# Linear attention and a leaky-ReLU FFN on one core: the four transposed tiles of one batch dealt out over two PSUM banks

## The chip, the cores and the metric

The kernel runs on one core of a Trainium2 chip. A time is the device time of one execution in microseconds (us), and the time of a kernel is the median of several executions. Beside these times there is one profiled execution, whose trace says for each instruction when it began, how long it took and what released it. All positions such as "73.66" are microseconds from the start of the span of that execution.

## The reference, cut to what matters

Eight batches of eight heads go through a linear attention (576 tokens, 64 features per head); the result, 4608 rows of 512 numbers, goes through two matrix products with a leaky ReLU between them.

```python
def phi(x, c, s):
    r = np.maximum(x, 0.0)
    return np.concatenate([r * c, r * s], axis=-1)
q_p, k_p = phi(q, cos_w, sin_w), phi(k, cos_w, sin_w)
kv = np.einsum('bhsf,bhsd->bhfd', k_p, v)
z = np.sum(k_p, axis=2)
num = np.einsum('bhsf,bhfd->bhsd', q_p, kv)
den = np.einsum('bhsf,bhf->bhs', q_p, z)[..., None] + 1e-06
x = (num / den).transpose(0, 2, 1, 3).reshape(B * S, H * D)
h = x @ w_in
out = np.maximum(0.01 * h, h) @ w_out
```

## The kernel before, in words

The rows are worked on in nine groups. Groups 0 to 7 are the first 512 tokens of the batches 0 to 7, as four tiles of 128 rows (`J = 4`); group 8 gathers the last 64 tokens of all batches. Group g = 2, the third batch, is the one that the change touches. For each group:

- the k and v of the batch are scaled (`k_token`, L253 on VectorE and GpSimd and L251 on ScalarE) and cast (`v_pairs`, L259 on ScalarE and L261 on the others), and `kv_sum` (L326) sums them into the 128x66 matrix of each head with 72 matmuls;
- `q_prep` scales q, a DMA transpose (L363) turns it;
- `num` (L412) multiplies tile j of q by these matrices into the PSUM tile `ps_num`, and `divide` (L423, L427, L428 on VectorE) divides and writes tile j of `xs`;
- `xs` is turned into `xT`, because the next product contracts over features. For groups 3 to 8 a DMA does it (L377). For group 2 TensorE does it, in `x_transpose(g, j, eng)`, tile by tile: four transposes of 128x128 (L389) write tile j of the PSUM tile `ps_x`, and a copy (L259, here always on ScalarE, since the entry `'xe'` of batch 2 is `'AAAA'`) brings it to `xT`;
- the first FFN product (L486 up to group 1; from group 2 on Strassen-like in seven products per unit, `ffn1s`, L638, whose sums of operands are made by `x_sum` and whose results are finished in `ffn1e`) and the second (`ffn2s`, L755, also in seven products, with sums of `g` made by `g_sum` on VectorE; all these sums have the line of the helper `tt_op`, L538).

The order of the work is written out by hand. `TUNE["O"]` is a string of units of matmuls per group, and every other step has a position on the same axis; `weave` issues a step as soon as its position is reached. What is issued after what on one engine is therefore fixed; the waits between engines are not in the code, they are derived from which instruction touches which tile. For group 2, `num` stands at positions 16.40, 17.14, 17.61 and 18.20 and `x_transpose` at 17.31, 17.68, 18.89 and 18.94. On TensorE the transposes of tile 0 to 3 (called X0 to X3 below, and their copies C0 to C3) therefore stand among the units of L755 of group 1 in this order: num 1, 4 matmuls, X0, 8 matmuls, num 2, X1, 12 matmuls, num 3, 12 matmuls, 4 matmuls, X2, X3, 12 matmuls, 4 matmuls, then the first unit of L638 of group 2.

Group 1's second FFN product runs its seven products in the order 1, 2, 6, 5, 7, 4, 3. After product 6 VectorE writes `t2` (L776), after product 7 `t3` (L778), both as a sum of a PSUM tile and `t1`; in the trace both are "ext<-ps,ext" of L538. Product 7 also needs `g_sum` number 3 ("g<-g" at 76.69), whose last part VectorE makes in this stage.

PSUM: the pool `ps_h` has two slots of two banks (a bank holds 2048 bytes per partition) for the tiles with the tag "h". `ps_x` is one of them, the chain of products 6 and 7 of group 1 another; after group 2's `x_transpose` the pool is closed, and its banks become the four tiles `ps_f0` to `ps_f3` of L638. A tile j of `ps_x` has 4 x 128 numbers of two bytes, 1024 bytes per partition, so `ps_x` fills two banks.

Of the kernel before, what the change touches and what calls it, by code (L numbers as in the profile page):

```python
# [9 lines left out]
dt = mybir.dt  # L10
# [3 lines left out]
P = 128  # L14
J = 4
# [5 lines left out]
def kernel(  # L21
# [26 lines left out]
    NKC = DM // P  # L48
# [29 lines left out]
    def psum(where, shape, dtype, name):  # L78
        p = {"h": ps_h, "o": ps_o, "n": ps_n}[where]
        return p.tile(shape, dtype, name=name, tag="ps_" + where)  # L80

    st = {}
# [5 lines left out]
    def need(*keys):  # L88
        for key in keys:
            assert key in done, key  # L90
# [166 lines left out]
    def copy(eng, o, i):  # L257
        if eng is ACT:
            nc.scalar.copy(o, i)  # L259
        else:  # L260
            eng.tensor_copy(o, i)  # L261
# [106 lines left out]
    def xT_tile(g):  # L368
        if ("xT", g) not in st:
            st["xT", g] = xtpool.tile([P, J, NKC, P], dt.float16, name="xT")  # L370
        return st["xT", g]
# [10 lines left out]
    def x_transpose(g, j, eng):  # L382

        need(("num", g, j))
        if j == 0:
            st["ps_x", g] = psum("h", [P, J, NKC, P], dt.float16, "ps_x")
        ps = st["ps_x", g][:, j]
        for c in range(NKC):
            nc.tensor.transpose(ps[:, c], st["xs", g][:, j, 2 * c : 2 * c + 2, :], ident)  # L389
        copy(eng, xT_tile(g)[:, j], ps)  # L390
        if j == J - 1:
            done.add(("xT", g))
# [488 lines left out]
    ps = psum("h", [P, 2, 512], dt.float32, "ps_numh")  # L881
# [81 lines left out]
    ps = psum("n", [P, 2, DM], dt.float32, "ps_o")  # L963
# [26 lines left out]
    ps = psum("h", [P, 2, MAIN], dt.float16, "ps_x")  # L990
# [177 lines left out]
    for b, t in TUNE["B"].items():  # L1168
# [17 lines left out]
        if isinstance(t["x"], list):  # L1186
            for j in range(J):
                at(t["x"][j], x_transpose, b, j, engines[t["xe"][j]])
        else:
            at(t["x"], x_transpose_dma, b)  # L1190
# [40 lines left out]
```

## Time and profile before

| | |
|---|---|
| median of 3 runs (lowest to highest) | 274.75 us (274.72 to 275.25) |
| the profiled execution, its own time | 275.64 us |
| its span, first instruction to last | 273.9 us |
| TensorE busy in the span | 264.3 us |
| VectorE busy | 209.3 us |
| ScalarE busy | 189.5 us |
| GpSimd busy | 114.1 us |
| granted TensorE clock, mean | 0.998 |

A row of the timeline reads: start in us, duration in us, engine, line, operation, output <- input, shape, number of instructions merged, and in brackets how long the engine sat idle before it and what ended that. PE is TensorE's matmuls, PEld its weight loads, DVE is VectorE, ACT is ScalarE, POOL is GpSimd, SPq the queue that issues most DMAs. Merged rows of matmuls carry the modelled end of the last one, which lies 0.1 to 0.2 us behind the start of the next row.

### The profile page before, as it was taken

What the parts mean: (1) busy time and instruction counts of PE and PEld (TensorE: products, weight loads), DVE (VectorE), ACT (ScalarE), POOL (GpSimd) and SP (SyncE); (2) the same over time, 40 slices, a digit from 0 to 9 for tenths busy, and PEclk for the clock granted to TensorE, in tenths of its full rate; (3) what the DMA queues carried; (4) which work ended last, traced back from release to release, by engine and by line L of the source; (5) the groups of instructions that cost most, each with busy time, mean ns of one, the idle gap of its engine ahead of it and who ended that gap; (6) DMA issues with size and microseconds to landing.
All of it is one profiled execution on the core that took longest, in us unless ns stands there. A gap on an engine that the chain in (4) does not pass through costs nothing.

```text
span 273.9 us, 7194 instructions
## 1 busy us (share of the span) xinstructions
PE 264.3 (97%) x2925; PEld 223.2 (81%) x2925; DVE 209.3 (76%) x430; ACT 189.5 (69%) x344; POOL 114.1 (42%) x93
## 2 busy tenths in 40 slices
PE   8799999999889999999999999999999999999994
PEld 3576555556779999999999999989999899999983
DVE  4760595698887899889797979886987778867652
ACT  7766537589968998988797878967857365645500
POOL 2496006992738818996693477330003001000000
PEclk9999999999999999999999999999999999999999
DMA  6999999989999499879979975847199051200314
GB/s 228 369 392 410 383 398 373 357 203 254 300 217 364 117 207 272 237 248 191 253 255 213 306 226 174 181 118 149 45 123 224 2 115 42 77 14 29 112 43 115
DMA packets 75040, 57.08 MB, mean 208 GB/s; under 512 B 47232, under 2 KB 63616, under 8 KB 74624
## 3 DMA queue, kind: packets, MB, share of 16 engines
q1 hardware_dynamic: 74400, 56.11, 73.8%
q10 hardware_dynamic: 608, 0.52, 0.6%
q8 instruction: 23, 0.38, 0.6%
q14 instruction: 9, 0.07, 0.1%
HBM read 36.70 MB, written 9.44 MB: 168 GB/s over the span
## 4 chain that ended last, share of the span: by engine, by line
PE 88%; DMA 3%; ACT 3%; DVE 1%; POOL 1%; SPq 1%; issue 1%; ACTq 0%
PE ps L755 32%; PE ps_f L638 31%; PE ps_h L486 10%; PE ps_o L512 5%; PE ps_kv L326 4%; DMA kst<-in_k_dram 3%; PE ps_num L412 3%; ACT qp L251 1%; PE ps_f L755 1%; POOL kp L253 1%; PE ps_qt L398 1%; ACT xT L259 1%; PE ps_xth L464 1%; PE ps_x L389 0%; SPq L135 0%
## 5 line engine op out<-in xcount | busy, mean ns | idle before, releaser
L755 PEld LDWEIGHTS <-g 128*128 128x128 f16 x640 | 61.5, 98 | 7.0 <-ACT g L665 0.2
L755 PE MATMUL ps<-w,g 128*128 128x256 f16 x496 | 65.4, 273 | 0.0
L665 ACT ACTIVATE g<-ps_f 128x512 f16<-128x512 f32 x84 | 48.3, 596 | 17.4 <-DVE ps_f L538 10.7
L638 PEld LDWEIGHTS <-w 128*128 128x128 f16 x448 | 48.7, 114 | 1.8 <-DVE ext L538 0.6
L638 PE MATMUL ps_f<-xT,w 128*128 128x256 f16 x336 | 48.7, 273 | 0.5 <-DVE ext L538 0.3
L638 PEld LDWEIGHTS <-wext 128*128 128x128 f16 x336 | 36.3, 114 | 0.7
L755 PE MATMUL ps<-T,ext 128*128 128x256 f16 x240 | 31.9, 273 | 0.0
L486 PE MATMUL ps_h<-xT,w 128*128 128x512 f16 (+1 forms) x144 | 28.9, 355 | 0.1
L253 POOL TENSOR_SCALAR kp<-kst,cos_t 128x256 f16<-128x256 f32 (+1 forms) x20 | 26.8, 1346 | 4.9 <-DMA kst<-in_k_dram 3.6
L755 PEld LDWEIGHTS <-ext 128*128 128x128 f16 x256 | 24.6, 98 | 2.6
L638 PE MATMUL ps_f<-X,wext 128*128 128x256 f16 x176 | 26.5, 273 | 0.0
L253 POOL TENSOR_SCALAR kp<-kst,sin_t 128x256 f16<-128x256 f32 x16 | 21.4, 1346 | 11.7 <-ACT ext L774 6.4
L486 PEld LDWEIGHTS <-w 128*128 128x128 f16 x144 | 16.0, 114 | 10.8
L538 DVE TENSOR_TENSOR ps_f<-ps_f,u 128x512 f32<-128x512 f32 x28 | 19.4, 694 | 6.4 <-ACT u L259 4.2
L538 DVE TENSOR_TENSOR y<-ps_f,s 128x512 f32<-128x512 f32 x28 | 19.2, 686 | 4.6 <-PE ps_f L638 3.4
L538 DVE TENSOR_TENSOR osb<-ps,ext 128x512 f32<-128x512 f32 x23 | 15.8, 687 | 7.2 <-PE ps L755 7.1
L259 ACT COPY u<-ps_f 128x512 f32<-128x512 f32 x25 | 14.7, 587 | 8.9 <-PE ps_f L638 8.6
L428 DVE TENSOR_TENSOR xs<-ps_num,rden 128x512 f16<-128x512 f32 x28 | 19.4, 691 | 1.0
L496 ACT ACTIVATE g<-ps_h 128x1024 f16<-128x1024 f32 x16 | 15.8, 1023 | 6.1 <-PE ps_h L486 6.1
L665 ACT ACTIVATE g<-y 128x512 f16<-128x512 f32 x28 | 17.7, 632 | 3.1 <-DVE y L538 3.1
L755 PE MATMUL ps<-ext,g 128*128 128x256 f16 x128 | 18.1, 273 | 0.0
L259 ACT COPY ps_f<-ps_f 128x512 f32<-128x512 f32 x24 | 13.7, 573 | 5.2 <-PE ps_f L638 4.5
(117 smaller groups left out, 464.4 us busy)
## 6 DMA issues: line engine op xcount, KB each, us to landing
out_dram<-osb SPq DMA_DIRECT2D x32, 256.0 KB, 2.8
qst<-in_q_dram SPq DMA_DIRECT2D x7, 1024.0 KB, 9.4
kst<-in_k_dram SPq DMA_DIRECT2D x6, 1152.0 KB, 9.5
vst<-in_v_dram SPq DMA_DIRECT2D x5, 1152.0 KB, 7.5
w2st<-in_moe_w_out_dram SPq DMA_DIRECT2D x3, 1024.0 KB, 11.9
vst<-in_v_dram SPq DMA_DIRECT2D x4, 576.0 KB, 8.0
ext<-in_moe_w_in_dram SPq DMA_DIRECT2D x4, 512.0 KB, 9.6
kst<-in_k_dram SPq DMA_DIRECT2D x2, 576.0 KB, 8.5
```

Of the source, the lines that this page charges most:

```text
L253: eng.tensor_scalar(out=o, in0=i, scalar1=0.0, scalar2=col, op0=ALU.max, op1=ALU.mult)
L259: nc.scalar.copy(o, i)
L326: nc.tensor.matmul(ps[:, o, (c - lo) * NE : (c - lo + 1) * NE], lhsT=st["kp", b][sl, c, j, :], rhs=vm[sl, c, j, :], start=(j == 0), stop=( ...
L412: nc.tensor.matmul(ps[lo:hi, h // 4, (h % 4) * NE : (h % 4 + 1) * NE], lhsT=qpT[:, h, lo:hi], rhs=kv[b][:, h, :],)
L428: nc.vector.tensor_tensor(out=xs, in0=ps[:, :, 0 : 4 * NE].rearrange("p a (b e) -> p a b e", e=NE)[:, :, :, 0:D], in1=rden.rearrange("p (a ...
L486: nc.tensor.matmul(ps[:, m % 2, lo:hi], lhsT=w1[m // 4, c][0][:, w1[m // 4, c][1], m % 4 : 512 : 4], rhs=xT[:, lo // P : hi // P, c, :], s ...
L496: nc.scalar.activation(st["g", g][:, m - 1 : m + 1, :], ps, AF.Lrelu)
L512: nc.tensor.matmul(st["ps_o", g, tt], lhsT=st["g", g][:, m, tt * P : (tt + 1) * P], rhs=w2[:, m, :], start=(m == 0), stop=(m == NFT - 1),)
L538: eng.tensor_tensor(out=o, in0=a, in1=b, op=op)
L638: nc.tensor.matmul(ps[:, mi * HT : (mi + 1) * HT], lhsT=a[:, c, 2 * r0 + mi : 512 : 4], rhs=b[:, c], start=(n in (1, 5) and mi == 0 and c ...
L665: nc.scalar.activation(st["g", g][:, m : m + 2, r * HT : (r + 1) * HT], {"a": A, "c": y22, "e": E, "d": B_}[e].rearrange("p (m t) -> p m t ...
L755: nc.tensor.matmul(ps[:, tt], lhsT=a[:, i, tt * P : (tt + 1) * P], rhs=b[:, i], start=(first and i == 0), stop=(i == NPR - 1 and (apart or ...
```

## The change

Two lines of `x_transpose` change. Tile j of `ps_x` was at offset j x 1024 bytes, so that tiles 0 and 1 lay in the first bank of its slot and tiles 2 and 3 in the second. It is now at bank j % 2, half j // 2: tiles 0 and 2 lie in the first bank, tiles 1 and 3 in the second. Size of the tile, instructions, their order and their engines stay as they were.

```diff
         if j == 0:
-            st["ps_x", g] = psum("h", [P, J, NKC, P], dt.float16, "ps_x")
-        ps = st["ps_x", g][:, j]
+            st["ps_x", g] = psum("h", [P, 2, J // 2, NKC, P], dt.float16, "ps_x")
+        ps = st["ps_x", g][:, j % 2, j // 2]
         for c in range(NKC):
             nc.tensor.transpose(ps[:, c], st["xs", g][:, j, 2 * c : 2 * c + 2, :], ident)
         copy(eng, xT_tile(g)[:, j], ps)
```

## The prediction

> **What bounds the kernel now.** I read the page first: the span, and the chain that ended last.
>
> ```profile
> span 273.9 us, 7194 instructions
> PE ps L755 32%; PE ps_f L638 31%; PE ps_h L486 10%; PE ps_o L512 5%; PE ps_kv L326 4%; DMA kst<-in_k_dram 3%; PE ps_num L412 3%; ACT qp L251 1%; PE ps_f L755 1%; POOL kp L253 1%; PE ps_qt L398 1%; ACT xT L259 1%; PE ps_xth L464 1%; PE ps_x L389 0%; SPq L135 0%
> ```
>
> The chain is TensorE nearly throughout; "ACT xT L259" with 1% is the copy out of `ps_x`, so the stage of the change lies on it. Next I took the timeline of TensorE there, and one row of its weight loads.
>
> ```profile
> 72.01 0.42 PE L412 MATMUL ps_num<-kv,qpT 128*128 128x66 f16 x8
> 73.66 0.38 PE L389 MATMUL ps_x<-ident,xs 128*128 128x128 f16 x4 [1.24 <-ACT xT L259]
> 73.88 1.47 PE L755 MATMUL ps<-T,ext 128*128 128x256 f16 x12
> 75.19 0.42 PE L412 MATMUL ps_num<-kv,qpT 128*128 128x66 f16 x8
> 75.45 1.47 PE L755 MATMUL ps<-T,ext 128*128 128x256 f16 x12
> 76.76 0.60 PE L755 MATMUL ps<-w,g 128*128 128x256 f16 x4
> 77.19 0.39 PE L389 MATMUL ps_x<-ident,xs 128*128 128x128 f16 x4
> 78.25 0.38 PE L389 MATMUL ps_x<-ident,xs 128*128 128x128 f16 x4 [0.67 <-ACT xT L259]
> ...
> 80.73 0.63 PE L638 MATMUL ps_f<-xT,w 128*128 128x256 f16 x4 [0.35 <-DVE ext L538]
> ...
> 82.16 1.32 PE L326 MATMUL ps_kv<-vm,kp 64*128 64x66 f16 x72
> ```
> ```profile
> 72.23 0.10 PEld L389 LDWEIGHTS <-xs 128*128 128x128 f16 x1
> ```
>
> Three gaps stand here. X1 (73.66) and X3 (78.25) wait for a copy on ScalarE, and the first unit of group 2 (80.73) waits for VectorE. The weights of X1 were loaded at 72.23, so its `xs` was ready 1.4 us before it ran: it waited for C0 alone, although C0 reads bytes that X1 doesn't write. X2 (77.19), the first tile of the other bank, didn't wait. That fits a wait per bank, though it doesn't prove one (rival B).
>
> ScalarE's rows say why the copies are late.
>
> ```profile
> 73.05 0.56 ACT L259 COPY xT<-ps_x 128x512 f16<-128x512 f16 x1
> ...
> 74.72 0.56 ACT L259 COPY xT<-ps_x 128x512 f16<-128x512 f16 x1
> ...
> 77.61 0.58 ACT L259 COPY xT<-ps_x 128x512 f16<-128x512 f16 x1 [1.52 <-PE ps_x L389]
> 78.67 0.58 ACT L259 COPY xT<-ps_x 128x512 f16<-128x512 f16 x1 [0.47 <-PE ps_x L389]
> ...
> 79.96 1.14 ACT L259 CAST vm<-vst 128x1152 f16<-128x1152 f32 x1
> ```
>
> C0 (73.05) and C1 (74.72) have no idle time ahead of them: they stand behind other work of ScalarE, which the change leaves where it is. C2 and C3 do wait, for X2 and X3. So the second half is a ping-pong: X2, C2, X3, C3, each after the other. VectorE's rows show what runs beside it.
>
> ```profile
> 73.51 0.58 DVE L253 TENSOR_SCALAR kp<-kst,sin_t 128x256 f16<-128x256 f32 x1
> 74.95 0.69 DVE L538 TENSOR_TENSOR ext<-ps,ext 128x512 f32<-128x512 f32 x1 [0.86 <-PE ps L755]
> ...
> 76.08 0.69 DVE L428 TENSOR_TENSOR xs<-ps_num,rden 128x512 f16<-128x512 f32 x1
> 76.69 0.41 DVE L538 TENSOR_TENSOR g<-g 128x512 f16<-128x512 f16 x1
> 77.03 1.22 DVE L538 TENSOR_TENSOR g<-g,ext 128x2048 f16<-128x2048 f16 x1
> 78.16 0.35 DVE L253 TENSOR_SCALAR kp<-kst,cos_t 128x256 f16<-128x256 f32 x1
> 79.29 0.42 DVE L538 TENSOR_TENSOR X<-xT 128x512 f16<-128x512 f16 x1 [0.78 <-ACT xT L259]
> 79.63 0.35 DVE L253 TENSOR_SCALAR kp<-kst,sin_t 128x256 f16<-128x256 f32 x1
> 79.98 0.69 DVE L538 TENSOR_TENSOR ext<-ps,ext 128x512 f32<-128x512 f32 x1
> ```
>
> VectorE is idle twice between 73.51 and 79.98: 0.86 us before `t2` (74.95), for the matmuls held up behind X1, and 0.78 us before the sum X (79.29), for C3. Then it makes `t3` (79.98), which frees the PSUM bank that the unit at 80.73 takes. The end of this stage is thus set by VectorE, and that is where the gain must be read, not at TensorE's gaps.
>
> **The change part by part.** Nothing is added or taken out, and no step is moved in any queue; only waits change. Removed: X1 after C0, X3 after C2. New: X2 after C0, X3 after C1.
>
> First gap. X1 follows num 2 at the pitch of num 3 and its successor (75.19 to 75.45, 0.26): 72.27 instead of 73.66, 1.39 earlier. The 12 matmuls behind it go to 72.49. `t2` began 1.07 behind their first (73.88 to 74.95), which would be 73.56, but VectorE is free only at 74.95 - 0.86 = 74.09. So `t2` moves by 0.86, not by 1.39. Behind it VectorE had no gap: xs 3 ends at 76.77 - 0.86 = 75.91, the sum of g (76.69) at 77.10 - 0.86 = 76.24.
>
> Second gap. TensorE's row: num 3 at 73.80, the 4 matmuls of product 7 (76.76) at 75.37, after `t2`'s end at 74.78. X2 follows at 77.19 - 1.39 = 75.80; its new wait, C0, ended at 73.61. X3 follows 0.22 later (73.66 to 73.88 is the pitch of four transposes) at 76.02: xs 3 is there at 75.91, and its new wait, C1, ended at 75.28, 0.74 earlier. Behind X3 stand 12 matmuls of product 7, at 76.24, then 4 more; their sum of g is there at 76.24. So the new waits cost nothing here, with 0.7 us to spare, and X3 comes 2.23 us earlier.
>
> What is late next. C2 starts 0.42 after X2 (77.19 to 77.61), at 76.22; ScalarE is free at 77.61 - 1.52 = 76.09. C3 starts at C2's end at the latest, 76.80, and ends at 77.38, before VectorE is through with the row at 78.16, which it left at 79.29 - 0.78 = 78.51 and would now leave at 77.65. The sum X then starts at 77.65 instead of 79.29: both idle times are gone, 0.86 + 0.78 = **1.64 us**. `t3` starts at 79.98 - 1.64 = 78.34; product 7's 12 matmuls end at 76.24 + 1.47 = 77.71, in time. The unit at 80.73 goes to 79.09. TensorE itself could have been 2.23 earlier; 0.59 of that becomes a longer wait for `t3`.
>
> Behind it. `kv_sum` (82.16) would go to 80.52. It needs the cast of v (79.96), which follows C3 by 1.29: 78.09 to 79.23. This half of v comes from a load that stands ahead of the change in SP's queue and doesn't move; the row behind it in that queue are q's transposes, and the last row is from the view of the DMA issues for this stretch (count, KB, us from issue to landing):
>
> ```profile
> 72.86 0.46 SPq L135 DMA_DIRECT2D vst<-in_v_dram  x1
> 73.49 5.77 SPq L363 DMA_TRANSPOSE qpT<-qp  x2
> ```
> ```profile
> vst<-in_v_dram SPq DMA_DIRECT2D x1, 576.0 KB, 4.5
> ```
>
> It lands at 72.86 + 4.5 = 77.36, 0.73 before the cast. From 82 on TensorE is full, and this row of the view by windows (its last three numbers are the granted clock, the DMA engines' busy share and GB/s) has the DMA engines 60% busy, so a backlog of loads that could not move up with the rest is worked off there:
>
> ```profile
> 86.00:92.00 6.00, 6.00 (x73) 5.48 (x71) 5.76 (x16) 5.64 (x12) 6.00 (x4) 1.00 0.60 230
> ```
>
> So the 1.64 us reach the end, bar what follows.
>
> The unknown cost is overlap with GpSimd. VectorE's sums move up into its last scaling of k:
>
> ```profile
> 75.70 1.13 POOL L253 TENSOR_SCALAR kp<-kst,sin_t 128x256 f16<-128x256 f32 x1
> ```
> ```profile
> 58.23 2.60 POOL L253 TENSOR_SCALAR kp<-kst,sin_t 128x256 f16<-128x256 f32 x1
> ```
> ```profile
> 58.45 1.21 DVE L538 TENSOR_TENSOR ext<-w,T 128x2048 f16<-128x2048 f16 x1
> ```
>
> At 58.45 VectorE took 1.21 for such a sum inside an operation of GpSimd, and 1.22 at 77.03 outside one; GpSimd's took 2.60 instead of 1.13. So GpSimd pays, and 75.70 + 2.60 = 78.30 is well before `kv_sum` at 80.52. But VectorE's scaling took 0.58 at 73.51 beside GpSimd and 0.35 at 78.16 alone, and the latter would now start at 77.30, possibly still beside it. Bounds: 0 (no overlap left) to 0.23 for that row, or 1.00 for the sum of g if it is held until GpSimd ends (75.70 + 1.13 = 76.83, instead of 76.69 - 0.86 = 75.83). A gain is excluded, since no operation of VectorE here gets less of GpSimd beside it than before. I take 0.10 in all, nearer to the pair at 58 us than to the upper ends.
>
> The Trainium skill speaks against this move: "SBUF — State Buffer", section "Who interferes with whom", says that a VectorE instruction with two SBUF inputs contends with a GpSimd one that reads SBUF, and that whichever issues second is blocked until the first is done. By it the sum of g would be the one held, and the gain would be that of rival A; the rows at 58 us show the opposite side paying.
>
> Writing one bank of `ps_x` while ScalarE reads the other is new as well, and no row shows it for this tile. If it cost nothing, the times above hold; if it cost everything, X1 would be held until C0's end and X3 until C2's, which is rival B's time. I take nothing: the two groups of 12 matmuls (73.88 and 75.45) both took 1.47, the first while C1 read another bank.
>
> Sum: 1.64 - 0.10 = **1.54 us**. The profiled execution, 275.64 with a span of 273.9, would become 274.1 with 272.4. It lies 0.89 above the median of the timed runs, and what lies around the span is not touched, so I take the difference over: 274.75 - 1.54 = **273.2 us**.
>
> **The rivals.**
>
> A, GpSimd's share. The sum of g is held by the scaling that began at 75.70, for 1.00. VectorE has no gap left to hide it, so the gain is 1.64 - 1.00 = 0.64, **274.1 us** (the 0.23 alone would leave 1.41, within the forecast). For it: the 0.58 at 73.51. Against it: the pair at 58 us, where the same kinds of operation met and VectorE lost nothing.
>
> B, the change doesn't do what it says. The waits are derived, and the trace before would look the same if they were per tile of PSUM: C1 ended at 75.28, so that X2 at 77.19 would have shown no wait for it either. Then X1 still waits for C0 and X3 for C2, and the time stays at **274.75 us**. For it: X1's wait is certainly coarser than the bytes. Against it: the bank is the next unit above the bytes, and every idle time of the stage is told by it.
>
> The Trainium skill's "PSUM — Partial Sum Buffer", section "PSUM bank collisions raise a hardware error", asks that PSUM be guarded by bank and quadrant and found two engines on different banks clean, so that a guard by whole tiles would be wider than needed; nothing in the trace tells which one was built here.
>
> C, slower: the half of v comes too late. The transposes of q stand right behind its load in SP's queue, and TensorE's own progress frees the buffer that the second one fills (`num` of group 2 reads it), so it may start up to 1.39 earlier and share the DMA engines with the load. A landing past 78.09 delays the cast; past 80.52 - 1.14 = 79.38 it delays `kv_sum` beyond its new time; the point from which the kernel is slower than before is a landing past 82.16 - 1.14 = 81.02, 8.2 us after its issue. Price, an estimate: shared half and half for its whole length the load takes 2 x 4.5 = 9.0, lands at 81.86, and `kv_sum` starts at 83.00, 0.84 late: **275.6 us**. For it: the two do overlap from 73.49 on. Against it: only 1.39 of the 4.5 can be newly shared, which ends at 78.75, not at 81.02.
>
> **How the numbers follow.** Forecast (a gain of 1.1 to 2.2): 0.68. A (0.55 to 1.1): 0.12. B: 0.10. C: 0.08. The remaining 0.02 is a gain above TensorE's own 2.23. The forecast's own range is 272.5 to 273.65, its ends being TensorE's 2.23 in place of VectorE's 1.64 and half of the 1.00 lost. For 8 in 10 A must be in: 272.4 to 274.2, with 0.1 below for the spread of a median. It leaves out B and C, 0.18. A measurement of this kernel can tell about 0.2%, 0.55 us, from no change. Faster by more than that: 0.68 + 0.12 + 0.02 = 0.82; within: B, 0.10; slower: C, 0.08.
>
> **What would show it.** Right: X1 and X3 with no idle time for "ACT xT" ahead of them, X1 about 0.26 behind num 2, C2 and C3 back to back, no longer each behind its transposes, VectorE without its 0.86 and 0.78, the wait for `t3` at the first L638 grown to about 0.9, that unit near 79.1 and `kv_sum` near 80.5. Wrong: waits at X1 or X3 as before (B); "g<-g" or the scalings of VectorE longer by tenths (A); an idle time of ScalarE for the DMA of v ahead of its cast (C). It would also be wrong if the gain stood at 80 us but was gone at the end: then a later stage, not this one, waits for something that didn't move up.

## The result: no measurable difference, and the same waits as before

| | before | changed |
|---|---|---|
| median (lowest to highest), 13 runs each | 275.15 us (274.72 to 275.94) | 274.99 us (274.67 to 275.64) |
| the profiled execution | 275.64 us | 274.91 us |
| its span | 273.9 us | 273.1 us |

The ratio is 0.9999, with a 95% interval of 0.9989 to 1.0008: the change is worth between 0.3 us faster and 0.2 us slower. The forecast of 273.2 us, with a range of 272.4 to 274.2, was wrong. The time is that of rival B. (B's own figure, 274.75, was the median of three runs; over 13 runs the kernel before came to 275.15.)

The timeline of the changed kernel shows it without any arithmetic. TensorE first, from X0 (70.20) to the first unit of group 2:

```profile
70.20 0.39 PE L389 MATMUL ps_x<-ident,xs 128*128 128x128 f16 x4
70.43 1.04 PE L755 MATMUL ps<-T,ext 128*128 128x256 f16 x8
71.30 0.42 PE L412 MATMUL ps_num<-kv,qpT 128*128 128x66 f16 x8
72.89 0.38 PE L389 MATMUL ps_x<-ident,xs 128*128 128x128 f16 x4 [1.17 <-ACT xT L259]
...
76.42 0.39 PE L389 MATMUL ps_x<-ident,xs 128*128 128x128 f16 x4
77.48 0.38 PE L389 MATMUL ps_x<-ident,xs 128*128 128x128 f16 x4 [0.67 <-ACT xT L259]
...
79.95 0.63 PE L638 MATMUL ps_f<-xT,w 128*128 128x256 f16 x4 [0.35 <-DVE ext L538]
```

X1 still sits idle for 1.17 us and X3 for 0.67, both released by "ACT xT", the copies. ScalarE's copies C0 and C3 of the same execution:

```profile
72.27 0.56 ACT L259 COPY xT<-ps_x 128x512 f16<-128x512 f16 x1
...
77.90 0.58 ACT L259 COPY xT<-ps_x 128x512 f16<-128x512 f16 x1 [0.47 <-PE ps_x L389]
```

C0 ends at 72.27 + 0.56 = 72.83 and X1 starts at 72.89, though X1 now writes the second bank and C0 reads the first. TensorE's 1.17 us of idle time began at 71.72, so that 0.55 us of it were over before C0 had begun (72.27). No conflict in PSUM can account for that part; a fixed order, X1 after C0, does. VectorE's two idle times, the terms of the forecast's sum, are there as before:

```profile
74.18 0.69 DVE L538 TENSOR_TENSOR ext<-ps,ext 128x512 f32<-128x512 f32 x1 [0.91 <-PE ps L755]
...
78.51 0.42 DVE L538 TENSOR_TENSOR X<-xT 128x512 f16<-128x512 f16 x1 [0.78 <-ACT xT L259]
```

From X0 to the first unit of L638 the stage takes 79.95 - 70.20 = 9.75 us. Before, X0 stood at

```profile
70.91 0.39 PE L389 MATMUL ps_x<-ident,xs 128*128 128x128 f16 x4
```

and the stage took 80.73 - 70.91 = 9.82. This length is used below for all kernels, since it is free of what happens ahead of X0 and behind the stage.

### The profile page after: what moved, and what is told of

Same layout as the page of the kernel before. It is cut to its first block, busy times and chain, and to the rows that moved or that the text cites. A ratio compares the mean times of both kernels' runs of the same rounds, so it can differ in the third digit from the quotient of the medians.

```text
span 273.1 us, 7194 instructions
## 1 busy us (share of the span) xinstructions
PE 263.2 (96%) x2925; PEld 222.9 (82%) x2925; DVE 209.2 (77%) x430; ACT 189.5 (69%) x344; POOL 114.8 (42%) x93
## 4 chain that ended last, share of the span: by engine, by line
PE 89%; DMA 3%; ACT 3%; DVE 1%; POOL 1%; SPq 1%; issue 1%; ACTq 0%
PE ps L755 33%; PE ps_f L638 32%; PE ps_h L486 10%; PE ps_o L512 5%; PE ps_kv L326 4%; DMA kst<-in_k_dram 3%; PE ps_num L412 3%; ACT qp L251 1%; PE ps_f L755 1%; POOL kp L253 1%; PE ps_qt L398 1%; ACT xT L259 1%; PE ps_xth L464 1%; PE ps_x L389 0%; SPq L135 0%
## 5 line engine op out<-in xcount | busy, mean ns | idle before, releaser
L755 PEld LDWEIGHTS <-g 128*128 128x128 f16 x640 | 61.5, 98 | 6.9 <-ACT g L665 0.2
L755 PE MATMUL ps<-w,g 128*128 128x256 f16 x496 | 65.4, 273 | 0.0
L638 PEld LDWEIGHTS <-w 128*128 128x128 f16 x448 | 48.7, 114 | 1.9 <-DVE ext L538 0.6
L638 PE MATMUL ps_f<-xT,w 128*128 128x256 f16 x336 | 48.8, 273 | 0.5 <-DVE ext L538 0.3
L638 PEld LDWEIGHTS <-wext 128*128 128x128 f16 x336 | 36.3, 114 | 0.7
L755 PE MATMUL ps<-T,ext 128*128 128x256 f16 x240 | 31.9, 273 | 0.0
L253 POOL TENSOR_SCALAR kp<-kst,cos_t 128x256 f16<-128x256 f32 (+1 forms) x20 | 25.9, 1303 | 4.1 <-DMA kst<-in_k_dram 2.8
L253 POOL TENSOR_SCALAR kp<-kst,sin_t 128x256 f16<-128x256 f32 x16 | 22.8, 1432 | 10.6 <-PE ps_kv L326 5.3
L755 PEld LDWEIGHTS <-ext 128*128 128x128 f16 x256 | 24.6, 98 | 2.5
L638 PE MATMUL ps_f<-X,wext 128*128 128x256 f16 x176 | 26.5, 273 | 0.0
L538 DVE TENSOR_TENSOR ps_f<-ps_f,u 128x512 f32<-128x512 f32 x28 | 19.4, 694 | 6.5 <-ACT u L259 4.3
L538 DVE TENSOR_TENSOR y<-ps_f,s 128x512 f32<-128x512 f32 x28 | 19.2, 687 | 4.8 <-PE ps_f L638 3.6
L538 DVE TENSOR_TENSOR osb<-ps,ext 128x512 f32<-128x512 f32 x23 | 15.8, 688 | 7.2 <-PE ps L755 7.1
L428 DVE TENSOR_TENSOR xs<-ps_num,rden 128x512 f16<-128x512 f32 x28 | 19.4, 692 | 1.0
L755 PE MATMUL ps<-ext,g 128*128 128x256 f16 x128 | 18.1, 273 | 0.0
```

Of the source, the lines that this page charges most:

```text
L253: eng.tensor_scalar(out=o, in0=i, scalar1=0.0, scalar2=col, op0=ALU.max, op1=ALU.mult)
L428: nc.vector.tensor_tensor(out=xs, in0=ps[:, :, 0 : 4 * NE].rearrange("p a (b e) -> p a b e", e=NE)[:, :, :, 0:D], in1=rden.rearrange("p (a ...
L538: eng.tensor_tensor(out=o, in0=a, in1=b, op=op)
L638: nc.tensor.matmul(ps[:, mi * HT : (mi + 1) * HT], lhsT=a[:, c, 2 * r0 + mi : 512 : 4], rhs=b[:, c], start=(n in (1, 5) and mi == 0 and c ...
L755: nc.tensor.matmul(ps[:, tt], lhsT=a[:, i, tt * P : (tt + 1) * P], rhs=b[:, i], start=(first and i == 0), stop=(i == NPR - 1 and (apart or ...
```

## The experiments

Two questions were open. Does the wait go with the tile of PSUM, or with something else? And was the rest of the prediction, what the waits are worth, sound? All kernels but the one before and the changed one take `ps_x` and the tile "ps_7" of products 6 and 7 from a pool `ps_m` that is opened for the purpose, so that two tiles of one bank each are possible:

```diff
+    def mid_pool():
+        early.close()
+        st["mid"] = early.enter_context(tc.tile_pool(name="ps_m", bufs=1, space=PS))
+        return st["mid"]
...
-                ps = psum(where, [P, 2, HC], dt.float32, "ps_7")
+                if where == "h":
+                    ps = st["mid"].tile([P, 2, HC], dt.float32, name="ps_7", tag="ps_y")
+                else:
+                    ps = psum(where, [P, 2, HC], dt.float32, "ps_7")
```

The added lines shift the profile's line numbers: L389 is L394 or L398 below, L412 is L417 or L421, L423 is L428 or L432, L638 is L643 or L647, L755 is L763 or L767, L538 is L543 or L547. What every kernel came to:

| kernel | where tiles 0 1 2 3 lie | waits at X1, X3 (us) | X0 to first L638 (us) | ratio to before (95%) |
|---|---|---|---|---|
| before | one tile, banks 0 0 1 1 | 1.24, 0.67 | 9.82 | 1 |
| changed | one tile, banks 0 1 0 1 | 1.17, 0.67 | 9.75 | 0.9999 (0.9989 to 1.0008) |
| pool_only | one tile, 0 0 1 1, `ps_m` | 1.10, 0.67 | 9.68 | 0.9991 (0.9982 to 1.0000) |
| one_alt | one tile, 0 1 0 1, `ps_m` | 1.10, 0.68 | 9.68 | 1.0002 (0.9989 to 1.0014) |
| two_pairs | two tiles, a a b b | 1.10, 0.67 | 9.68 | 0.9990 (0.9976 to 1.0004) |
| first_only | two tiles, a b b b | none, 0.67 | 8.43 | 0.9951 (0.9938 to 0.9963) |
| second_only | two tiles, a a a b | 1.09, none | 9.02 | 0.9971 (0.9960 to 0.9981) |
| two_alt | two tiles, a b a b | none, none | 7.76 | 0.9931 (0.9918 to 0.9943) |
| two_alt_again | the same kernel | none, none | 7.76 | 0.9936 (0.9921 to 0.9952) |
| two_alt_s4 | the same, one sum of VectorE later | none, none | 7.76 | 0.9944 (0.9922 to 0.9966) |

### two_alt: two tiles, dealt out as the change meant it

```diff
-            st["ps_x", g] = psum("h", [P, J, NKC, P], dt.float16, "ps_x")
-        ps = st["ps_x", g][:, j]
+            mid = mid_pool()
+            st["ps_x", g] = [
+                mid.tile([P, 2, NKC, P], dt.float16, name=f"ps_x{i}", tag=f"ps_x{i}")
+                for i in range(2)
+            ]
+        ps = st["ps_x", g][[0, 1, 0, 1][j]][:, [0, 0, 1, 1][j]]
```

> Two PSUM tiles of one bank each in place of the one tile of two banks, dealt out as the change meant it: tiles 0 and 2 of the batch to the first, 1 and 3 to the second. Theory (the derived wait is per PSUM tile, not per bank; the rest of the prediction holds): X1 runs 0.26 us behind num 2 without a wait for C0, X3 0.22 us behind X2 without a wait for C2, VectorE loses its idle times of 0.86 and 0.78, and the kernel is 1.5 us faster than before (1.1 to 1.7). Rival 1 (X1 and X3 wait for something else than the tile of PSUM, so that the waits stay): no change, 0.0. Rival 2 (the waits go, but a later stage takes the gain back): first unit of L638 about 1.6 us earlier, the end within 0.3 us of before.

Measured: 273.13 us against 275.00 of before beside it, and 273.18 against 275.05 the second time: 1.9 us faster both times, and above the expected 1.1 to 1.7. TensorE, in the first of the two profiles:

```profile
70.64 0.39 PE L398 MATMUL ps_x<-ident,xs 128*128 128x128 f16 x4
...
71.73 0.42 PE L421 MATMUL ps_num<-kv,qpT 128*128 128x66 f16 x8
71.99 0.38 PE L398 MATMUL ps_x<-ident,xs 128*128 128x128 f16 x4
...
75.52 0.61 PE L398 MATMUL ps_x<-ident,xs 128*128 128x128 f16 x8
75.97 1.47 PE L767 MATMUL ps<-w,g 128*128 128x256 f16 x12
77.28 0.60 PE L767 MATMUL ps<-ext,g 128*128 128x256 f16 x4
78.40 0.63 PE L647 MATMUL ps_f<-xT,w 128*128 128x256 f16 x4 [0.52 <-DVE ext L547]
```

X1 stands 0.26 behind num 2 and has no bracket; X2 and X3 are merged into one row of 8 transposes (75.52), since nothing lies between them. The only wait left is that for `t3`, at the first unit, grown from 0.35 to 0.52, not to the 0.9 of the prediction. Otherwise this is the picture that the prediction had asked for, in another kernel. Rival 1 is out, and so is rival 2: the 1.9 us are still there at the end.

### one_alt: the same banks, one tile

```diff
-            st["ps_x", g] = psum("h", [P, J, NKC, P], dt.float16, "ps_x")
-        ps = st["ps_x", g][:, j]
+            st["ps_x", g] = mid_pool().tile([P, 2, J // 2, NKC, P], dt.float16, name="ps_x", tag="ps_x")
+        ps = st["ps_x", g][:, j % 2, j // 2]
```

> The layout of the change in one tile of two banks, taken from the pool that two_alt opens: every instruction, address and bank is that of two_alt, and only the waits can differ. Theory (the derived wait is per tile of PSUM): X1 waits about 1.1 us for C0 and X3 0.67 us for C2, as in the control pool_only, and the time is that of pool_only, 0.0 to 0.3 us under before, 1.6 to 1.9 above two_alt. Rival (the banks or addresses matter to the chip, or the pool does): it comes out near two_alt, 1.5 us or more under before.

Measured: 275.02 us against 275.05. The view of TensorE's waits for this stage (us in total, times, longest):

```profile
PE ps_x L394 <- ACT xT L259: 1.8, 2, 1.1
PE ps_f L643 <- DVE ext L543: 0.3, 1, 0.3
```

This is the closest pair of the study: by their code one_alt and two_alt have the same instructions in the same order and deal the tiles out over the banks alike (the views show no addresses), and they differ in whether the two banks belong to one tile or to two. The two waits, and 1.84 us of the time, go with the tile. Whether the chip would slow a write to one bank of `ps_x` while ScalarE reads the other is hardly tested by this, because in two_alt the two scarcely meet. These are C0, and C2 with C3 in one row, in two_alt:

```profile
72.63 0.57 ACT L259 COPY xT<-ps_x 128x512 f16<-128x512 f16 x1
...
75.95 1.07 ACT L259 COPY xT<-ps_x 128x512 f16<-128x512 f16 x2 [0.26 <-PE ps_x L398]
```

X1's row is over at 71.99 + 0.38 = 72.37, before C0 begins, and the row with X3 in it ends at 75.52 + 0.61 = 76.13, less than 0.2 us after C2 begins.

### two_pairs: two tiles, filled two by two

In two_alt's diff the last line becomes `st["ps_x", g][[0, 0, 1, 1][j]][:, [0, 1, 0, 1][j]]`.

> Two tiles of one bank each, but filled two by two as in before: 0 and 1 in the first, 2 and 3 in the second. Theory: X1 shares its tile with C0 and X3 with C2, so both waits stay, and X2 loses a wait that cost nothing: no gain over the control pool_only, within 0.3 us of it. Rival (two tiles alone bring the gain, the alternation nothing): 1.6 us faster than before.

Measured: 274.71 us against 275.05, and the same two waits:

```profile
PE ps_x L398 <- ACT xT L259: 1.8, 2, 1.1
PE ps_f L647 <- DVE ext L547: 0.3, 1, 0.3
```

Two tiles alone bring nothing: both the second tile and the alternation are needed. The change made the second without the first.

### first_only and second_only: one wait at a time

In two_alt's diff the last line becomes `st["ps_x", g][[0, 1, 1, 1][j]][:, [0, 0, 1, 0][j]]` and `st["ps_x", g][[0, 0, 0, 1][j]][:, [0, 1, 0, 0][j]]`.

> Two PSUM tiles of one bank, tile 0 of the batch alone in the first, 1 to 3 in the second: takes away only the wait of X1 for C0. Theory, worked out with the rows of before: X2 at 75.80, C2 ends at 76.80, X3 still waits for C2 and runs at 76.84, C3 ends at 77.84, the sum X starts at 77.88 instead of 79.29: 1.4 us faster, so nearly all of the gain. Rival 1: 0.0. Rival 2: 0.0 at the end.

> Two PSUM tiles of one bank, tiles 0 to 2 of the batch in the first, 3 alone in the second: takes away only the wait of X3 for C2. Theory: X1 waits for C0 as before, X3 at 77.41 instead of 78.25, C3 ends at 78.77, VectorE is through at 78.51, the sum X starts at 78.79 instead of 79.29: 0.5 us faster. If the two gaps added up instead, it would be 0.8. Rivals 1 and 2: 0.0.

Measured: 273.61 and 274.11 us against 275.00, so 1.35 (1.02 to 1.70) and 0.80 (0.52 to 1.10) faster by the ratios. The first meets the expected 1.4. The second lies above the expected 0.5, at the 0.8 that was named for the case that the gaps add up. In first_only's timeline X1 runs at once, X3 still waits for C2:

```profile
71.72 0.38 PE L398 MATMUL ps_x<-ident,xs 128*128 128x128 f16 x4
...
76.31 0.38 PE L398 MATMUL ps_x<-ident,xs 128*128 128x128 f16 x4 [0.67 <-ACT xT L259]
```

Against the control's 9.68 us the stage is 1.25 shorter in first_only, 0.66 in second_only and 1.92 in two_alt. 1.25 + 0.66 = 1.91: in the stage, the two waits are worth what they add up to. The first is worth more than half although VectorE hides part of it, because it moves C2, X3 and C3 up as well. Second_only's 0.66 is 0.16 more than its working gave. Its sum X came 1.53 us after X2 began (76.41 to 77.94) where 1.60 was taken, and `t3` 0.60 after the sum X where 0.69 was taken.

### pool_only: the control

The diff of `mid_pool` alone, with `ps_x` as one tile of two banks from it.

> Control: the one tile of two banks as before, but taken from the pool that the other runs open for the purpose (the old pool is closed one step earlier). All theories: no change, within 0.3 us, X1 and X3 waiting 1.2 and 0.7 us as before. If it is faster or slower, the pool and not the tiles moves the other runs.

Measured: 274.84 us against 275.00, ratio 0.9991 (0.9982 to 1.0000). The two ends of the stage on TensorE, 9.68 us apart, and the waits in it:

```profile
70.66 0.39 PE L394 MATMUL ps_x<-ident,xs 128*128 128x128 f16 x4
...
73.27 0.38 PE L394 MATMUL ps_x<-ident,xs 128*128 128x128 f16 x4 [1.10 <-ACT xT L259]
...
77.86 0.38 PE L394 MATMUL ps_x<-ident,xs 128*128 128x128 f16 x4 [0.67 <-ACT xT L259]
...
80.34 0.63 PE L643 MATMUL ps_f<-xT,w 128*128 128x256 f16 x4 [0.35 <-DVE ext L543]
```

So at most 0.5 us of the other runs' gains can be the pool's, by the interval, and one_alt, with the same pool, gained nothing (1.0002). In the stage the pool is worth 9.82 - 9.68 = 0.14 us.

### two_alt_s4: what ends the stage once the waits are gone

```diff
-     'S4': 18.8521,
+     'S4': 19.45,
```

> two_alt with the sum number 4 of g (VectorE, 1.21 us, needed only by the last product) issued after t3 and the sum X instead of before them. What sets the end of the stage in two_alt: VectorE is through with its queue at 77.05, and C3 ends at 77.02, so both arrive together. Theory 1 (the chain X3, C3, sum X, t3 is next, 0.03 us behind): no gain over two_alt, within 0.3 us; VectorE idles about 1.1 us ahead of the sum X. Theory 2 (VectorE's queue alone sets the end): t3 up to 0.2 us earlier, when product 7 ends, and the rest of the 1.1 us unused; 0.2 us faster.

Measured: 273.28 us, against 273.18 of two_alt in the same session, and the same 7.76 us of the stage. ScalarE's C2 and C3 (one row) and VectorE's sum X, with 1.2 us of work taken out of its way:

```profile
77.63 1.07 ACT L259 COPY xT<-ps_x 128x512 f16<-128x512 f16 x2 [0.26 <-PE ps_x L398]
```
```profile
78.73 0.42 DVE L547 TENSOR_TENSOR X<-xT 128x512 f16<-128x512 f16 x1 [1.05 <-ACT xT L259]
```

C3 ends at 78.70; VectorE now waits 1.05 us for it and starts the sum no earlier. So in two_alt the chain X2, C2, C3, sum X, `t3` ends the stage, and VectorE's queue is only level with it.

## Why the prediction was wrong, point by point

**What bounds the stage: right.** X1 waits for C0, X3 for C2, and both cost time at the end: taking them away gave 1.9 us.

**The step that failed** stands at the head of "the change part by part": "Removed: X1 after C0, X3 after C2." It was inferred from "X2 (77.19), the first tile of the other bank, didn't wait. That fits a wait per bank". X2's lack of idle time was no evidence, as rival B said: C1 had ended at 75.28, 1.9 us before X2 came, so that a wait for it could not show. For `ps_x` in this kernel the derived waits are as wide as the tile of PSUM: X1 waits for a copy that reads neither its bytes nor its bank (changed, one_alt), and stops waiting as soon as its bank is a tile of its own (two_alt). The prediction gave this 0.10. With no row on either side of the question, it should have had about as much as the forecast, and the range should have reached past 274.75. The argument "the bank is the next unit above the bytes" was an argument from names and not from the profile.

The Trainium skill's "PSUM — Partial Sum Buffer", section "PSUM bank collisions raise a hardware error", was cited beside rival B: it says what a guard needs to cover, and the derived guard here covers more. Its finding that two engines on different banks run clean is hardly touched by these runs, since X3 and C2 of two_alt overlap by less than 0.2 us.

**The size of the gain, had the waits gone: the mechanism right, 1.54 for 1.9.** The term that was mis-sized is VectorE's bound of 1.64. In the prediction's times VectorE was through with its work ahead of the sum X at 77.65 and C3 ended at 77.38, which is 6.74 and 6.47 us after X0 (70.91). VectorE was thus to set the end of the stage. In two_alt VectorE runs without a marked idle time from the scaling at 73.23 to `t3`:

```profile
73.23 0.34 DVE L253 TENSOR_SCALAR kp<-kst,sin_t 128x256 f16<-128x256 f32 x1
73.49 0.68 DVE L547 TENSOR_TENSOR ext<-ps,ext 128x512 f32<-128x512 f32 x1
74.09 0.15 DVE L432 TENSOR_SCALAR den<-ps_num 128x8 f32<-128x8 f32 x1
...
75.13 0.52 DVE L547 TENSOR_TENSOR g<-g 128x512 f16<-128x512 f16 x1
75.57 1.21 DVE L547 TENSOR_TENSOR g<-g,ext 128x2048 f16<-128x2048 f16 x1
76.71 0.34 DVE L253 TENSOR_SCALAR kp<-kst,cos_t 128x256 f16<-128x256 f32 x1
77.05 0.43 DVE L547 TENSOR_TENSOR X<-xT 128x512 f16<-128x512 f16 x1
77.39 0.35 DVE L253 TENSOR_SCALAR kp<-kst,sin_t 128x256 f16<-128x256 f32 x1
77.66 0.68 DVE L547 TENSOR_TENSOR ext<-ps,ext 128x512 f32<-128x512 f32 x1
```

It is ready for the sum X at 77.05, and C3 ends at 75.95 + 1.07 = 77.02: 6.41 and 6.38 us after X0 (70.64). C3 came as worked out, to 0.09 us, and VectorE 0.33 earlier. In the second profile of the same kernel VectorE was even the first to be ready, at 76.20 + 0.35 = 76.55; C3 ended at 75.54 + 1.07 = 76.61, and the sum X followed at 76.64:

```profile
75.54 1.07 ACT L259 COPY xT<-ps_x 128x512 f16<-128x512 f16 x2 [0.26 <-PE ps_x L398]
```
```profile
76.20 0.35 DVE L253 TENSOR_SCALAR kp<-kst,cos_t 128x256 f16<-128x256 f32 x1
76.64 0.43 DVE L547 TENSOR_TENSOR X<-xT 128x512 f16<-128x512 f16 x1
```

The stage took 7.76 us both times. So what set its length was the chain of C3, as two_alt_s4 says too, with VectorE's queue level with it in the first profile and ahead in the second.

Where the 2.06 us of the stage (9.82 - 7.76) come from can be read in VectorE's rows, counted from X0. `t2` comes after 2.85 us (70.64 to 73.49) instead of 4.04 (70.91 to 74.95), 1.19 less: the idle 0.86 and another 0.33. From `t2` to the sum X it is 3.56 instead of 4.34, the idle 0.78. From there to `t3` it is 0.61 instead of 0.69. That is 2.05; the medians give 1.9. The two idle times were measured as they stood, and 0.41 came on top. Of this, 0.24 is the scaling ahead of `t2`, with 0.34 instead of 0.58. The rest is mostly that `t2` and `t3` now begin 0.08 before the row ahead of them ends. Before, `t3` (79.98) began 0.04 behind the end of product 7's 12 matmuls (78.47 + 1.47 = 79.94), so that it was probably held by them: a third wait, too short for a bracket.

The prediction had excluded a gain on this side, since no operation of VectorE would get less of GpSimd beside it. In two_alt the scaling did not get less: it lies wholly inside GpSimd's row

```profile
71.50 2.32 POOL L253 TENSOR_SCALAR kp<-kst,cos_t 128x256 f16<-128x256 f32 x2
```

and took 0.34 all the same. So GpSimd beside it is not enough to explain the 0.58 of before, and what does explain it stays open.

**Rival A, overlap with GpSimd: 0.11 and 0.01 us, and neither reached the end.** GpSimd's scaling of k and VectorE's sum of g, in the second profile of two_alt:

```profile
74.17 1.13 POOL L253 TENSOR_SCALAR kp<-kst,sin_t 128x256 f16<-128x256 f32 x1
```
```profile
74.74 0.42 DVE L547 TENSOR_TENSOR g<-g 128x512 f16<-128x512 f16 x1
```

In the first profile GpSimd's row was

```profile
74.91 1.13 POOL L253 TENSOR_SCALAR kp<-kst,sin_t 128x256 f16<-128x256 f32 x1
```

and the sum of g began at 75.13, inside it, and took 0.52 instead of 0.41. Both are far from the upper bound of 1.00, and the stage took 7.76 us with either, so that the 0.10 of the prediction's sum was not paid. In the first profile, `t2` was followed after 0.60 us (73.49 to 74.09) and not after 0.70 as before, which made up for the 0.11. GpSimd paid nothing, 1.13 as before, where the prediction had allowed for 2.60. At 58 us two scalings of q on VectorE (57.92 and 59.58) met GpSimd's row as well as the sum did, so that the 2.60 there need not have been the sum's doing. The Trainium skill's rule of the shared port, cited from "SBUF — State Buffer", section "Who interferes with whom", would have held the sum until 76.04. It ended at 75.65, so this run does not show the rule, and for this pair the measurement decides.

**Rival C, the half of v:** ScalarE's cast of it ran in two_alt without a wait,

```profile
77.71 1.15 ACT L259 CAST vm<-vst 128x1152 f16<-128x1152 f32 x1
```

and the load of this half landed at 72.59 + 4.3 = 76.89, 0.8 us before the cast began. It took 4.3 us where it had taken 4.5, so q's transposes behind it did not slow it more than before:

```profile
72.59 0.46 SPq L135 DMA_DIRECT2D vst<-in_v_dram  x1
```
```profile
vst<-in_v_dram SPq DMA_DIRECT2D x1, 576.0 KB, 4.3
```

**What would show it** served its purpose: "waits at X1 or X3 as before (B)" is what the first rows of the changed kernel say.

## What to carry to other kernels

Before counting a wait as gone, find the thing that creates it, and a row that tells its width from the next wider one; an instruction that didn't wait tells nothing if what it might have waited for was long over. Compare too when a wait began with when the work that ended it began: TensorE stood still 0.55 us for a copy that had not started, which is the mark of a fixed order and not of a conflict. Where the derived waits are as wide as the tile, as here, moving data inside a tile changes no wait: to let a producer run ahead of a consumer, give the two halves tiles of their own and alternate between them, which here was worth about 0.65% (ratios 0.9931 and 0.9936, two_alt) while the alternation alone was worth nothing. When waits that alternate with copies go, work out the whole chain and not the gaps of one engine, for the first of them also moved everything behind it.

## What the runs showed of the hardware that was not expected

One and the same scaling on VectorE (128x256, from k) took from 0.34 (two_alt, 73.23) to 0.83 us. The latter is in one_alt, where it met GpSimd's cast of v:

```profile
74.34 0.83 DVE L253 TENSOR_SCALAR kp<-kst,sin_t 128x256 f16<-128x256 f32 x1
```
```profile
73.89 1.14 POOL L261 CAST vm<-vst 128x1152 f16<-128x1152 f32 x1
```

It ended at 75.17, just behind the cast at 75.03, as if held by it; in two_alt the same scaling and the sum of g, both begun inside a scaling of GpSimd, were not held. The runs don't tell which property of the two operations decides, and it cost one_alt nothing, since VectorE waited for TensorE behind it anyway.
